# Four gate products and a second weight conversion moved into the attention loop of a fused attention and two-layer expert kernel

## The chip, the cores and the metric

The kernel runs on one core of a Trainium2 chip, as one program. The metric is the device time of one execution in microseconds. The engines are TensorE (PE, with its weight loads as PEld), VectorE (DVE), ScalarE (ACT), GpSimd (POOL) and SyncE (SP), whose queue issues the transfers.

## What is computed

Attention with rotary positions over 2 x 8 heads of 576 tokens and 64 dimensions, then a gated layer (512 to 1536 and back) over the 1152 tokens, then eight experts (512 to 1024 and back), all of them run for every token and weighted by a matrix that is normalised by rows and columns in turn.

```python
q_rot, k_rot = rotate(q), rotate(k)
attn = softmax(q_rot @ k_rot^T / 8)
x = heads_to_tokens(attn @ v)                      # 1152 x 512

g = x @ w_gate                                     # 512 x 1536
x = (g * sigmoid(g) * (x @ w_val)) @ w_out         # back to 1152 x 512

P = exp(x @ moe2_w_gate - max)                     # 1152 x 8
for _ in range(8):
    P /= P.sum(1); P /= P.sum(0); P *= 1152 / 8
out = sum(P[:, e] * (relu(x @ w1[e]) @ w2[e]) for e in range(8))
```

## The kernel before

Everything is float32. Each operand of a large product is split into a high part (rounded to the format that PE multiplies fast) and a low part (what the rounding left), and `mm3` (L145) issues three matmuls for one product: high by high (L148), high weights by low activations (L149), low weights by high activations (L150). Splitting the gated layer's weights is the work of `convert` (L103): a transfer on SP's queue (L114), an absolute value on ACT (L120), two DVE steps (L122, L123), a third (L126), the high part on ACT (L129), two more on DVE (L130, L132), and a subtraction (L66) and an addition (L136) that finish the low part. Outside attention all of a 1024-column unit goes at once and the last two are DVE's; inside attention it goes in halves of 512 columns, and the last two are POOL's.

**Attention** takes the heads in eight pairs, four for each batch. A pair has nine steps, one for each tile of scores: step 9n + u computes the scores of tile u of pair n (`scores`, L257), and DVE takes their row maximum (`row_max`, L262). One step later ACT takes the exponential (`exps`, L278), two steps later PE transposes it (`turn`, L297), which DVE or ACT copies out (`turned`, L312). The products with the values (`values`, L364) of the first four tiles and of the last five follow at steps given by `VALUES`, as do `rest`, `inverse` and `spread`, which turn the remainders and the inverse row sums. `summed` (L373) multiplies the two on DVE, and `finish` splits the result into `xh` (ACT, L379) and `xl` (L66). A dictionary `plan` keeps each of these calls under a step and a slot; `SLOTS` is the order of the slots within one step, and the steps run from -1 to 80. PE, ACT, POOL and SP execute the calls in this order; DVE's order is left to the scheduler. The last scores are those of step 71; the steps from 72 to 80 finish the last pair. Scores lie in a PSUM pool `ps_s` of two tiles with two banks each; transposes and values have two banks each, in `ps_t` and `ps_v`.

**Conversions in attention.** `CONVERSIONS` gives the step at which each half unit of the gate weights begins. Its load stands four steps before, and its stages 0 to 8 steps after:

```python
CONVERSIONS = (18, 32)
for i, t0 in enumerate(CONVERSIONS):
    f, half = divmod(i, 2)
```

So unit 0 is converted within attention, one half at step 18 and the other at step 32.

**The gated layer** (`gated`) has twelve units `f` of 128 columns, with gate and value weights side by side, and three chunks `c` of 384 tokens. `gv(f, c)` computes the gate product `pg` and the value product `pv`, 4 x 3 matmuls each, in two banks of a pool `ps` with eight, which is opened when attention's pools are closed. ACT takes the SiLU (L520), DVE the product with `pv` (L521), ACT the high part `uh` (L522) and DVE the low part `ul` (L66). Units 1 and 2 are converted first, and unit f + 2 when unit f begins. The output products `po` follow, and then the experts: `w1_tile` (12 matmuls, read by L591 on ACT and L592 on DVE) and `w2_tile`. The order of these instructions on each engine is the scheduler's, by its own estimate of times.

Of the kernel before, what the change touches and what calls it, by code (L numbers as in the profile page):

```python
# [10 lines left out]
F32 = mybir.dt.float32  # L11
# [5 lines left out]
PSUM = bass.MemoryType.PSUM  # L17
# [5 lines left out]
CH = 384  # L23
NC = NT // CH
KD = DM // 128
# [19 lines left out]
VALUES = ((1, 1, 3, 4, 4), (1, 2, 2, 4, 4))  # L45
SUMMED = (7, 6)
ACT_TURNS = (0, 2, 6)
CONVERSIONS = (18, 32)
WARM = 20
SCALE = float(1.0 / np.sqrt(D))  # L50

# [5 lines left out]
def fused(ctx, tc, qk, v, rope, wgv, wo, wg2, w1, w2, out):  # L57
    nc = tc.nc

    def pool(name, bufs=1, space=None, stack=ctx, **kw):  # L60
        if space is not None:
            kw["space"] = space
        return stack.enter_context(tc.tile_pool(name=name, bufs=bufs, **kw))
# [75 lines left out]
    def load_w64(src):  # L139
        hi, lo = new_w()  # L140
        for _ in convert(src, hi, lo, wide=True):
            pass
        return hi, lo

    def mm3(ps, w, wsl, x, xsl, first, last):  # L145
        wh, wl = w
        xh, xl = x
        nc.tensor.matmul(ps, wh[wsl], xh[xsl], start=first, stop=False)  # L148
        nc.tensor.matmul(ps, wh[wsl], xl[xsl], start=False, stop=False)  # L149
        nc.tensor.matmul(ps, wl[wsl], xh[xsl], start=False, stop=last)  # L150


    def attention(xT, W):
        with ExitStack() as st:
            inp.append(pool("inp", bufs=2, stack=st))
            ap_ = pool("att", stack=st)
# [5 lines left out]
            pt = pool("pt", bufs=1, stack=st)  # L162
            sm = pool("sm", bufs=4, stack=st)
            xf_p = pool("xf", bufs=2, stack=st)
            ps_s = pool("ps_s", bufs=2, space=PSUM, stack=st)
            ps_t = pool("ps_t", bufs=2, space=PSUM, stack=st)
            ps_v = pool("ps_v", bufs=2, space=PSUM, stack=st)

# [272 lines left out]
            for i, t0 in enumerate(CONVERSIONS):  # L441
# [6 lines left out]
                    at(t0 + t, slot, next, parts_)  # L448
                at(t0 + 8, "pool", next, parts_, None)


            first, later, half = slice(0, 256), slice(256, S), 288
            for x in blocks:
# [42 lines left out]
            assert not plan  # L496


    def gated(x, x2, ps, W, W1):
        nonlocal cvp  # L500
        with ExitStack() as st:
            cvp = pool("cvp", bufs=2, stack=st)
            up = pool("up", stack=st)
            tp = pool("tp", bufs=2, stack=st)
            uh = [up.tile([128, NT], F32R, name=f"uh{f}") for f in range(KF)]
            ul = [up.tile([128, NT], F32R, name=f"ul{f}") for f in range(KF)]

            def gv(f, c):
                if f not in W:
                    W[f] = load_w64(wgv[f])  # L510
                w = W[f]
                ts = slice(c * CH, c * CH + CH)
                pg = ps.tile([128, 512], F32, tag="a", name="pg")[:, 0:CH]
                pv = ps.tile([128, 512], F32, tag="a", name="pv")[:, 0:CH]
                for o, dst in ((0, pg), (512, pv)):
                    for kk in range(KD):
                        mm3(dst, w, (slice(None), slice(o + kk * 128, o + kk * 128 + 128)),
                            x, (slice(None), kk, ts), kk == 0, kk == KD - 1)
                sg = tp.tile([128, CH], F32, tag="sg", name="sg")
                nc.scalar.activation(out=sg, in_=pg, func=AF.Silu)  # L520
                nc.vector.tensor_tensor(out=sg, in0=pv, in1=sg, op=ALU.mult)  # L521
                nc.scalar.copy(out=uh[f][:, ts], in_=sg)  # L522
                sub(ul[f][:, ts], sg, uh[f][:, ts])

            order = [(f, c) for f in range(KF) for c in range(NC)]
            for f in range(2):
                if f not in W:
                    W[f] = load_w64(wgv[f])
            for n, (f, c) in enumerate(order):
                if c == 0 and f + 2 < KF and f + 2 not in W:  # L530
                    W[f + 2] = load_w64(wgv[f + 2])
                gv(f, c)
            O = {}
            nc.sync.dma_start(out=wr, in_=wg2)
            nc.scalar.copy(out=wg[:, :, 0], in_=wr)
            sub(wg[:, :, 1], wr, wg[:, :, 0])

            def o_unit(i):
                if i * 8 < KD * KF and i not in O:
                    O[i] = load_w64(wo[:, i * WU:(i + 1) * WU])  # L540

            o_unit(0)
            o_unit(1)
            xh, xl = x2
            for d in range(KD):
                for c in range(NC):
                    if d == KD - 1 and c < 2:
                        W1[0, c] = load_w(w1[0, :, c * WU:(c + 1) * WU])
                    ts = slice(c * CH, c * CH + CH)
                    po = ps.tile([128, 512], F32, tag="a", name="po")[:, 0:CH]  # L550
                    for kk in range(KF):
                        i, o = divmod(d * KF + kk, 8)
                        o_unit(i + 1)
                        mm3(po, O[i], (slice(None), slice(o * 128, o * 128 + 128)),
                            (uh[kk], ul[kk]), (slice(None), ts), kk == 0, kk == KF - 1)
                    nc.scalar.copy(out=xh[:, d, ts], in_=po)
                    sub(xl[:, d, ts], po, xh[:, d, ts])


    def experts(x, ps, W1):  # L560
        nonlocal cvp
        cvp = None
        inp.append(pool("inp", bufs=4))
# [17 lines left out]

        def w1_tile(e, c, f, hh, hl):
            ts = slice(c * CH, c * CH + CH)
            po = ps.tile([128, 512], F32, tag="a", name="p1")[:, 0:CH]
            i, o = divmod(f, 2)
            for kk in range(KD):
                q = o * 512 + kk * 128
                mm3(po, W1[e, i], (ALLP, slice(q, q + 128)), x, (ALLP, kk, ts), kk == 0, kk == KD - 1)
                if e == 0:
                    gate_step()  # L590
            nc.scalar.activation(out=hh[:, f], in_=po, func=AF.Relu)  # L591
            nc.vector.scalar_tensor_tensor(out=hl[:, f], in0=po, scalar=0.0, in1=hh[:, f].bitcast(F32),  # L592
                                           op0=ALU.max, op1=ALU.subtract)

        def w2_tile(e, c, t, hh, hl):
            po = ps.tile([128, 512], F32, tag="a", name="p2")
            tl = slice(t * 128, t * 128 + 128)
            for f in range(KF2):
                i, o = divmod(f, 2)
                wh, wl = W2[e, i]  # L600
                ws = slice(o * 512, o * 512 + 512)
                nc.tensor.matmul(po, hh[:, f, tl], wh[:, ws], start=f == 0, stop=False)  # L602
                nc.tensor.matmul(po, hh[:, f, tl], wl[:, ws], start=False, stop=False)  # L603
                nc.tensor.matmul(po, hl[:, f, tl], wh[:, ws], start=False, stop=f == KF2 - 1)  # L604
            t = c * 3 + t
            if e == 0:
                nc.vector.tensor_scalar(out=acc[:, t], in0=po, scalar1=Pm[:, t, e:e + 1], scalar2=None, op0=ALU.mult)
            else:
                nc.vector.scalar_tensor_tensor(out=acc[:, t], in0=po, scalar=Pm[:, t, e:e + 1], in1=acc[:, t],  # L609
                                               op0=ALU.mult, op1=ALU.add)  # L610
            if e == E - 1:
                nc.sync.dma_start(out=out[t * 128:t * 128 + 128, :], in_=acc[:, t])

        def gate():
# [2 lines left out]
            lt = ep.tile([2 * E, NT], F32, name="lt")  # L617
            for c in range(NC):
                ts = slice(c * CH, c * CH + CH)
                pl = ps.tile([128, 512], F32, tag="a", name="plt")  # L620
                for kk in range(KD):
                    nc.tensor.matmul(pl[0:2 * E, 0:CH], wgf[:, kk], xh[:, kk, ts], start=kk == 0, stop=False)
                    nc.tensor.matmul(pl[0:2 * E, 0:CH], wgf[:, kk], xl[:, kk, ts], start=False, stop=kk == KD - 1)
                nc.scalar.copy(out=lt[:, ts], in_=pl[0:2 * E, 0:CH])
                yield
            pt = ps.tile([128, 512], F32, tag="a", name="pt")
            for t in range(NTT):
                nc.tensor.transpose(pt[:, t * 16:t * 16 + 16], lt[:, t * 128:t * 128 + 128], ident[0:16, 0:16])
            lg = ep.tile([128, NTT, E], F32, name="lg")
# [2 lines left out]
            mx = ep.tile([128, 1], F32, name="mx")  # L632
            nc.vector.tensor_reduce(out=mx, in_=lg, axis=AX.XY, op=ALU.max)
            yield
            pm = ps.tile([128, 512], F32, tag="a", name="pm")
            nc.tensor.transpose(pm[0:1, 0:128], mx, ident)
            m1 = ep.tile([1, 1], F32, name="m1")
            nc.vector.tensor_reduce(out=m1, in_=pm[0:1, 0:128], axis=AX.X, op=ALU.max, negate=True)
            yield
            pb = ps.tile([128, 512], F32, tag="a", name="pb")  # L640
            nc.tensor.matmul(pb[:, 0:1], ones[0:1, :], m1, start=True, stop=True)
            nb = ep.tile([128, 1], F32, name="nb")
            nc.vector.tensor_copy(out=nb, in_=pb[:, 0:1])
# [4 lines left out]
            for _ in range(8):  # L648
# [2 lines left out]
                nc.vector.reciprocal(out=rs, in_=rs)  # L651
                nc.vector.tensor_tensor(out=Pm, in0=Pm, in1=rs.unsqueeze(2).to_broadcast([128, NTT, E]), op=ALU.mult)
                yield
                pc = ps.tile([128, 512], F32, tag="a", name="pc")
                nc.tensor.matmul(pc[:, 0:NTT * E], ones, Pm.rearrange("p t e -> p (t e)"), start=True, stop=True)
                nc.vector.tensor_reduce(out=cs, in_=pc[:, 0:NTT * E].rearrange("p (t e) -> p e t", e=E),
                                        axis=AX.X, op=ALU.add)
# [41 lines left out]

    make_identity(nc, ident)  # L700
    nc.gpsimd.memset(ones, 1.0)
    xT = new_x()
    W = {}
    attention(xT, W)
    ps = pool("ps", bufs=8, space=PSUM)
    x2 = new_x()
    W1 = {}
    gated(xT, x2, ps, W, W1)
    experts(x2, ps, W1)


# [54 lines left out]
```

## Time and profile before

| | us |
|---|---|
| runs | 1208.04, 1212.86, 1212.77 |
| median of the runs | 1212.77 |
| profiled execution | 1212.68 |
| its span, first to last instruction | 1210.60 |
| PE busy in the span | 1193.5 |
| DVE busy | 542.0 |
| ACT busy | 334.7 |
| POOL busy | 90.5 |

Busy time of PE is from the start of a matmul to its modelled end, and these overlap from one matmul to the next. So the time of one matmul in a row of them is read from the distance of their starts. A busy share is a mean over stages; what a stage waits for is read from the waits and from the order of time in that stage. Attention ends at about 178 us, the gated layer at about 407, and the rest is the experts.

### The profile page before, as it was taken

The numbers are of one execution on the slowest core, as the hardware profiler recorded it, in microseconds if no ns is written. First come the engines' busy times: TensorE is split into PE (matmuls) and PEld (weight loads), VectorE is DVE, ScalarE is ACT, GpSimd is POOL, SyncE is SP. The second block draws the span as 40 slices with busy tenths as digits, with TensorE's granted clock in tenths as the row PEclk, the third lists the DMA queues.
The fourth block names the chain that finished last, engine by engine and source line by source line (L and its number), as shares of the span: only waits on it lengthen the run. The fifth ranks groups of instructions, "written<-read, shape, count | busy, mean of one in ns | idle before, by whom it ended". The sixth has DMA issues, their size and how long they took to land.

```text
span 1210.6 us, 15264 instructions
## 1 busy us (share of the span) xinstructions
PE 1193.5 (99%) x6456; PEld 1074.7 (89%) x6456; DVE 542.0 (45%) x850; ACT 334.7 (28%) x599; POOL 90.5 (7%) x86
## 2 busy tenths in 40 slices
PE   7999999999999999999999999999999999999998
PEld 6666669999999999899899999989989989998997
DVE  7699868998742453232232332332323233233221
ACT  4556544443411412121131221212202112122110
POOL 5468400000000000000000000000000000000000
PEclk7899999999999999999999999999999999999999
DMA  4767503332211301010120220210102012020001
GB/s 158 207 163 187 144 25 116 120 125 87 88 53 57 135 1 53 30 58 19 52 70 1 70 70 1 70 68 3 49 22 70 15 56 70 1 70 1 9 18 52
DMA packets 24115, 80.52 MB, mean 67 GB/s; under 512 B 4272, under 2 KB 4784, under 8 KB 21872
## 3 DMA queue, kind: packets, MB, share of 16 engines
q1 hardware_dynamic: 24048, 79.56, 21.2%
q8 instruction: 50, 0.82, 0.3%
q14 instruction: 17, 0.14, 0.0%
HBM read 64.80 MB, written 2.36 MB: 55 GB/s over the span
## 4 chain that ended last, share of the span: by engine, by line
PE 94%; DVE 4%; DMA 1%; ACT 1%; issue 0%; SPq 0%; DVEq 0%; ACTq 0%
PE p L148 11%; PE p L150 11%; PE p L149 11%; PE p L603 11%; PE p L604 11%; PE p L602 11%; PE s L257 4%; PE pv L364 3%; PE t L297 2%; PE po L150 2%; PE po L149 2%; PE po L148 2%; PE pg L150 2%; PE pg L148 2%; PE pv L150 2%; PE pg L149 2%
## 5 line engine op out<-in xcount | busy, mean ns | idle before, releaser
L148 PE MATMUL p<-xh,wh 128*128 128x384 f32 x768 | 257.7, 336 | 0.0
L150 PE MATMUL p<-xh,wl 128*128 128x384 f32 x768 | 256.8, 334 | 0.0
L149 PE MATMUL p<-xl,wh 128*128 128x384 f32 x768 | 256.7, 334 | 0.0
L604 PE MATMUL p<-wh,hl 128*128 128x512 f32 x576 | 224.4, 390 | 0.0
L603 PE MATMUL p<-wl,hh 128*128 128x512 f32 x576 | 224.4, 390 | 0.0
L602 PE MATMUL p<-wh,hh 128*128 128x512 f32 x576 | 224.0, 389 | 0.0
L591 ACT ACTIVATE hh<-p 128x384 fp32r<-128x384 f32 x192 | 94.2, 491 | 370.6 <-PE p L150 370.6
L592 DVE SCALAR_TENSOR_TENSOR hl<-p,hh 128x384 fp32r<-128x384 f32 x192 | 106.8, 556 | 188.7 <-ACT hh L591 188.6
L609 DVE SCALAR_TENSOR_TENSOR acc<-p,Pm,acc 128x512 f32<-128x512 f32 x63 | 47.3, 750 | 254.1 <-PE p L604 254.1
L148 PEld LDWEIGHTS p<-xh,wh 128*128 128x128 f32 x768 | 144.2, 188 | 0.9
L149 PEld LDWEIGHTS p<-xl,wh 128*128 128x128 f32 x768 | 144.2, 188 | 0.6
L150 PEld LDWEIGHTS p<-xh,wl 128*128 128x128 f32 x768 | 144.1, 188 | 0.0
L99 ACT CAST wh<-raw 128x1024 fp32r<-128x1024 f32 x64 | 67.2, 1053 | 249.3 <-PE p L604 197.7
L604 PEld LDWEIGHTS p<-wh,hl 128*128 128x128 f32 x576 | 108.1, 188 | 22.5
L603 PEld LDWEIGHTS p<-wl,hh 128*128 128x128 f32 x576 | 108.1, 188 | 22.2
L602 PEld LDWEIGHTS p<-wh,hh 128*128 128x128 f32 x576 | 108.1, 188 | 22.1
L66 DVE TENSOR_TENSOR wl<-raw,wh 128x1024 fp32r<-128x1024 f32 x64 | 78.2, 1224 | 78.4 <-ACT wh L99 76.5
L262 DVE TENSOR_REDUCE ng<-s 128x1 f32<-128x576 f32 x72 | 53.5, 749 | 15.6 <-PE s L257 10.6
L278 ACT ACTIVATE p<-s,ng 128x576 f32<-128x576 f32 x64 | 47.6, 743 | 40.1 <-DVE ng L262 39.8
L148 PE MATMUL pg<-xh,wh 128*128 128x384 f32 x144 | 48.9, 339 | 3.1 <-ACT wh L129 2.4
L149 PE MATMUL pg<-xl,wh 128*128 128x384 f32 x144 | 48.5, 337 | 0.0
L150 PE MATMUL pg<-xh,wl 128*128 128x384 f32 x144 | 48.5, 337 | 0.0
(126 smaller groups left out, 1400.6 us busy)
## 6 DMA issues: line engine op xcount, KB each, us to landing
raw<-in_w SPq DMA_DIRECT2D x64, 512.0 KB, 3.9
raw<-in_wgv SPq DMA_DIRECT2D x11, 1024.0 KB, 4.9
x<-in_qk SPq DMA_DIRECT2D x15, 576.0 KB, 4.6
raw<-in_wo SPq DMA_DIRECT2D x6, 1024.0 KB, 4.9
x<-hl SPq DMA_DIRECT2D x42, 144.0 KB, 3.4
x<-hl SPq DMA_DIRECT2D x14, 288.0 KB, 3.3
v<-in_v SPq DMA_DIRECT2D x8, 320.0 KB, 5.0
out<-acc SPq DMA_DIRECT2D x9, 256.0 KB, 2.0
```

Of the source, the lines that this page charges most:

```text
L66: (eng or nc.vector).tensor_tensor(out=out_, in0=a, in1=hi.bitcast(F32), op=ALU.subtract)
L99: nc.scalar.copy(out=hi, in_=raw)
L148: nc.tensor.matmul(ps, wh[wsl], xh[xsl], start=first, stop=False)
L149: nc.tensor.matmul(ps, wh[wsl], xl[xsl], start=False, stop=False)
L150: nc.tensor.matmul(ps, wl[wsl], xh[xsl], start=False, stop=last)
L257: nc.tensor.matmul(ps[:, c, o:o + ks.stop - ks.start], q, k, start=t == 0, stop=t == len(terms) - 1)
L262: nc.vector.tensor_reduce(out=R[n, u], in_=SC[n, u][:, :, 0:288], axis=AX.XY, op=ALU.max, negate=True)
L591: nc.scalar.activation(out=hh[:, f], in_=po, func=AF.Relu)
L592: nc.vector.scalar_tensor_tensor(out=hl[:, f], in0=po, scalar=0.0, in1=hh[:, f].bitcast(F32), op0=ALU.max, op1=ALU.subtract)
L602: nc.tensor.matmul(po, hh[:, f, tl], wh[:, ws], start=f == 0, stop=False)
L603: nc.tensor.matmul(po, hh[:, f, tl], wl[:, ws], start=False, stop=False)
L604: nc.tensor.matmul(po, hl[:, f, tl], wh[:, ws], start=False, stop=f == KF2 - 1)
```

## The change

Two more conversions stand in the loop, so unit 1 of the gate weights is converted at steps 50 and 63 of attention. At steps 72 to 75 a new function `gate_half` is planned in the slot `pe3`; it computes the gate and the value product of chunk 0 for unit 0 (72 and 73) and for unit 1 (74 and 75). Their results lie in score tiles: the score pool is now `duos`, opened before attention and kept until the end. The gated layer's other banks are a pool `singles` of four, opened when attention's pools are closed, and `bank` hands out its banks and the halves of `duos` tiles in turn. In `gated`, the results of chunk 0 of units 0 and 1 are read first; then unit f + 2 is converted when unit f begins, and units 0 and 1 compute chunks 1 and 2 alone. All other places that took a bank of `ps` now call `bank`.

```diff
-CONVERSIONS = (18, 32)
+CONVERSIONS = (18, 32, 50, 63)
+AHEAD = (72, 73, 74, 75)
...
-            ps_s = pool("ps_s", bufs=2, space=PSUM, stack=st)
+            ps_s = duos
...
+            for i, t0 in enumerate(AHEAD):
+                at(t0, "pe3", gate_half, xT, W, G, *divmod(i, 2))
...
+    def gate_half(x, W, G, f, half):
+
+        if half == 0:
+            G[f] = duos.tile([128, 2, 512], F32, tag="s", name="g")
+        for kk in range(KD):
+            o = half * 512 + kk * 128
+            mm3(G[f][:, half, 0:CH], W[f], (slice(None), slice(o, o + 128)), x, (slice(None), kk, slice(0, CH)),
+                kk == 0, kk == KD - 1)
...
             def gv(f, c):
-                if f not in W:
-                    W[f] = load_w64(wgv[f])
-                w = W[f]
                 ts = slice(c * CH, c * CH + CH)
-                pg = ps.tile([128, 512], F32, tag="a", name="pg")[:, 0:CH]
-                pv = ps.tile([128, 512], F32, tag="a", name="pv")[:, 0:CH]
-                for o, dst in ((0, pg), (512, pv)):
-                    for kk in range(KD):
-                        mm3(dst, w, (slice(None), slice(o + kk * 128, o + kk * 128 + 128)),
-                            x, (slice(None), kk, ts), kk == 0, kk == KD - 1)
+                if c == 0 and f in G:
+                    pg, pv = (G[f][:, i, 0:CH] for i in range(2))
+                else:
+                    w = W[f]
+                    pg, pv = bank("pg")[:, 0:CH], bank("pv")[:, 0:CH]
+                    for o, dst in ((0, pg), (512, pv)):
+                        for kk in range(KD):
+                            mm3(dst, w, (slice(None), slice(o + kk * 128, o + kk * 128 + 128)),
+                                x, (slice(None), kk, ts), kk == 0, kk == KD - 1)
...
-            order = [(f, c) for f in range(KF) for c in range(NC)]
-            for f in range(2):
-                if f not in W:
-                    W[f] = load_w64(wgv[f])
-            for n, (f, c) in enumerate(order):
-                if c == 0 and f + 2 < KF and f + 2 not in W:
+            for f in G:
+                gv(f, 0)
+            for f in range(KF):
+                if f + 2 < KF:
                     W[f + 2] = load_w64(wgv[f + 2])
-                gv(f, c)
+                for c in range(int(f in G), NC):
+                    gv(f, c)
...
+    duos = pool("duos", bufs=2, space=PSUM)
+    singles = duo = None
+    turns = [0]
+
+    def bank(name):
+
+        nonlocal duo
+        i = turns[0] % 8
+        turns[0] += 1
+        if i < 4:
+            return singles.tile([128, 512], F32, tag="a", name=name)
+        if i % 2 == 0:
+            duo = duos.tile([128, 2, 512], F32, tag="s", name=name)
+        return duo[:, i % 2]
+
     xT = new_x()
-    W = {}
-    attention(xT, W)
-    ps = pool("ps", bufs=8, space=PSUM)
+    W, W1, G = {}, {}, {}
+    attention(xT, W, G)
+    singles = pool("singles", bufs=4, space=PSUM)
```

## Rows read from the trace of the kernel before

**Rows 1.** The page, part 1: busy us, share of the span, instructions

```profile
PE 1193.5 (99%) x6456; PEld 1074.7 (89%) x6456; DVE 542.0 (45%) x850; ACT 334.7 (28%) x599; POOL 90.5 (7%) x86
```

**Rows 2.** Waits of PE over the span: in total, times, longest

```profile
PE s L257 <- ACT hl L209: 5.1, 1, 5.1
PE pg L148 <- ACT wh L129: 2.4, 1, 2.4
```

**Rows 3.** PE in order of time: start, us, operation, idle time before it

```profile
178.21 0.41 PE L148 MATMUL pg<-xh,wh 128*128 128x384 f32 x1 [0.68 <-DVE xf L373]
...
190.79 0.33 PE L148 MATMUL pg<-xh,wh 128*128 128x384 f32 x1
...
192.69 0.34 PE L149 MATMUL pv<-xl,wh 128*128 128x384 f32 x1
195.47 0.69 PE L148 MATMUL pg<-xh,wh 128*128 128x384 f32 x1 [2.44 <-ACT wh L129]
...
198.66 0.33 PE L150 MATMUL pg<-xh,wl 128*128 128x384 f32 x1
```

**Rows 4.** Stretches: PE, PEld, DVE, ACT, POOL busy, granted clock, DMA share, GB/s

```profile
170.00:178.20 8.20, 7.52 (x48) 3.65 (x49) 4.27 (x12) 2.15 (x7) 1.41 (x1) 1.00 0.00 0
195.10:198.40 3.30, 2.93 (x9) 2.94 (x10) 3.30 (x5) 0.73 (x2) 0.00 (x0) 0.50 0.44 104
```

**Rows 5.** Order of time: the first load behind attention, the low parts on DVE

```profile
178.21 18.08 SPq L114 DMA_DIRECT2D raw<-in_wgv  x3
...
194.72 1.21 DVE L136 TENSOR_TENSOR wl<-cv,raw 128x1024 fp32r<-128x1024 f32 x1
...
199.31 1.23 DVE L136 TENSOR_TENSOR wl<-cv,raw 128x1024 fp32r<-128x1024 f32 x1
```

**Rows 6.** Order of time: the last exponential, PE's `values` behind it

```profile
170.48 0.75 ACT L278 ACTIVATE p<-s,ng 128x576 f32<-128x576 f32 x1
...
171.64 0.65 PE L364 MATMUL pv<-q,v 64*64 64x256 f32 x4
```

**Rows 7.** Order of time: the half conversion of step 32, first and last

```profile
91.19 0.68 ACT L120 ACTIVATE cv<-raw 128x512 f32<-128x512 f32 x1
...
109.06 1.33 POOL L136 TENSOR_TENSOR wl<-cv,raw 128x512 fp32r<-128x512 f32 x1
```

**Rows 8.** Order of time: PE and weight loads where tile shapes change

```profile
157.96 0.76 PE L364 MATMUL pv<-p,v 128*64 128x320 f32 x4
158.65 0.80 PE L257 MATMUL s<-x,x 128*128 128x288 f32 x4
...
160.20 1.30 PE L364 MATMUL pv<-p,v 128*64 128x320 f32 x8
161.43 0.40 PE L257 MATMUL s<-hl,bd 128*128 128x288 f32 x1
...
173.93 0.20 PEld L349 LDWEIGHTS t<-ident,iv 128*128 128x128 f32 x2 [0.49 <-issue]
```

**Rows 9.** Stretches as in 4: attention's pairs 1 to 6

```profile
41.45:59.69 18.24, 18.24 (x129) 12.80 (x127) 14.75 (x28) 11.37 (x26) 9.03 (x9) 1.00 0.65 174
59.69:79.74 20.05, 18.82 (x129) 12.83 (x127) 19.26 (x33) 11.48 (x27) 12.83 (x11) 1.00 0.62 161
79.74:99.85 20.11, 18.99 (x132) 12.95 (x131) 19.49 (x34) 11.95 (x28) 14.67 (x13) 1.00 0.72 198
99.85:116.92 17.07, 17.07 (x125) 12.44 (x126) 14.17 (x30) 11.84 (x28) 12.07 (x11) 1.00 0.65 175
116.92:135.71 18.79, 18.29 (x128) 12.77 (x127) 15.88 (x29) 11.74 (x28) 13.96 (x13) 1.00 0.61 156
135.71:153.96 18.25, 18.25 (x129) 12.80 (x127) 14.93 (x28) 10.55 (x25) 4.63 (x5) 1.00 0.44 104
```

**Rows 10.** Groups of instructions: busy us, mean ns, idle before

```profile
L521 DVE TENSOR_TENSOR sg<-pv,sg 128x384 f32<-128x384 f32 x35 | 19.4, 553 | 11.0 <-PE pv L150 10.9
L592 DVE SCALAR_TENSOR_TENSOR hl<-p,hh 128x384 fp32r<-128x384 f32 x192 | 106.8, 556 | 188.7 <-ACT hh L591 188.6
```

More of the change, by code (lines that the diff above doesn't have):

```diff
@@ L150, in mm3, with attention @@
         nc.tensor.matmul(ps, wl[wsl], xh[xsl], start=False, stop=last)
-    def attention(xT, W):
+    def attention(xT, W, G):
         with ExitStack() as st:
@@ L496, in attention, with gated @@
             assert not plan
-    def gated(x, x2, ps, W, W1):
+    def gate_half(x, W, G, f, half):
[5 more added lines that the diff above has]
+                kk == 0, kk == KD - 1)
+    def gated(x, x2, W, W1, G):
         nonlocal cvp
@@ L549, in gated @@
                     ts = slice(c * CH, c * CH + CH)
-                    po = ps.tile([128, 512], F32, tag="a", name="po")[:, 0:CH]
+                    po = bank("po")[:, 0:CH]
                     for kk in range(KF):
@@ L557, in gated, with experts @@
                     sub(xl[:, d, ts], po, xh[:, d, ts])
-    def experts(x, ps, W1):
+    def experts(x, W1):
         nonlocal cvp
@@ L583, in w1_tile @@
             ts = slice(c * CH, c * CH + CH)
-            po = ps.tile([128, 512], F32, tag="a", name="p1")[:, 0:CH]
+            po = bank("p1")[:, 0:CH]
             i, o = divmod(f, 2)
@@ L595, in w2_tile @@
         def w2_tile(e, c, t, hh, hl):
-            po = ps.tile([128, 512], F32, tag="a", name="p2")
+            po = bank("p2")
             tl = slice(t * 128, t * 128 + 128)
@@ L619, in gate @@
                 ts = slice(c * CH, c * CH + CH)
-                pl = ps.tile([128, 512], F32, tag="a", name="plt")
+                pl = bank("plt")
                 for kk in range(KD):
@@ L625, in gate @@
                 yield
-            pt = ps.tile([128, 512], F32, tag="a", name="pt")
+            pt = bank("pt")
             for t in range(NTT):
@@ L634, in gate @@
             yield
-            pm = ps.tile([128, 512], F32, tag="a", name="pm")
+            pm = bank("pm")
             nc.tensor.transpose(pm[0:1, 0:128], mx, ident)
@@ L639, in gate @@
             yield
-            pb = ps.tile([128, 512], F32, tag="a", name="pb")
+            pb = bank("pb")
             nc.tensor.matmul(pb[:, 0:1], ones[0:1, :], m1, start=True, stop=True)
@@ L653, in gate @@
                 yield
-                pc = ps.tile([128, 512], F32, tag="a", name="pc")
+                pc = bank("pc")
                 nc.tensor.matmul(pc[:, 0:NTT * E], ones, Pm.rearrange("p t e -> p (t e)"), start=True, stop=True)
@@ L701, in fused @@
     nc.gpsimd.memset(ones, 1.0)
+    duos = pool("duos", bufs=2, space=PSUM)
[10 more added lines that the diff above has]
+        return duo[:, i % 2]
     xT = new_x()
-    W = {}
-    attention(xT, W)
-    ps = pool("ps", bufs=8, space=PSUM)
+    W, W1, G = {}, {}, {}
+    attention(xT, W, G)
+    singles = pool("singles", bufs=4, space=PSUM)
     x2 = new_x()
-    W1 = {}
-    gated(xT, x2, ps, W, W1)
-    experts(x2, ps, W1)
+    gated(xT, x2, W, W1, G)
+    experts(x2, W1)
 def _tables():
```

## Prediction

> **What bounds the kernel now.** I read the page's busy shares first: TensorE (PE) is busy for 99% of the span, VectorE (DVE) for 45% [rows 1]. So only what PE waits for, or what is added to its stream, moves the end. The list of PE's waits comes next: one of 5.1 us at the start, which the change doesn't touch, then 2.4 us in the gate products for `wh` from ScalarE (ACT) [rows 2]; the others are smaller. The third view is the order of time on PE around the 2.4 us. Unit 0 of the gate weights, converted during attention, gives PE 72 products from 178.21 to 190.79, which is 0.1747 us each. Then come 12 products of unit 1 that need only its high part, then nothing until 195.47, 2.44 us after the last had ended [rows 3]. [...] So the ten products from 195.47 to 198.66 take 3.19 us [rows 3] and not 1.75. The gap with its slow clock costs 2.44 + 1.44 = **3.88 us**.
>
> What PE stands for is the conversion of units 1 and 2. Its first transfer is issued at 178.21, when attention's last result is out. Unit 1's low part is written by 194.72 + 1.21 = 195.93 and unit 2's by 199.31 + 1.23 = 200.54, which is 17.7 and 22.3 us after that issue [rows 5].
>
> The last main view is the stretch in which the change puts the first products, the end of attention. It would pay to put them there if PE were idle. PE is busy 7.52 of 8.20 us [rows 4], and the only wait of size is the 0.68 us at 178.21 for DVE's last product [rows 3].
>
> **The change part by part.** *Products moved into attention.* Four half products of 12 matmuls, 4 x 12 x 0.1747 = 8.39 us of PE time, move from behind 178.21 to steps 72 to 75. The same 48 matmuls go on the same engine, which has no gaps there: moved alone they cost and bring nothing, and attention ends 8.39 us later. DVE's and ACT's work in those steps (copies of turned probabilities, inverse sums) runs beside them. The 0.68 us wait stays, I take it: the new pool of four banks lies where attention's other PSUM pools were, and can wait for the same last reader. If it goes, 0.68 us are won.
>
> New waits on PE: a score tile must be free, and `wl` of unit 1 must be written. Behind a waiting product stand the next `turn`, `rest` and `values` on PE, and behind those DVE's copies. The last exponential is over at 170.48 + 0.75 = 171.23, and the first product comes behind the `values` that start at 171.64 [rows 6]: both tiles are free in time. For `wl`, the slower of the earlier halves took from 91.19 to 110.39, from its first ACT to the end of its last POOL instruction, 19.2 us [rows 7]. The second half of unit 1 starts at step 63, whose scores lie near 154 [rows 9], so it is done near 173; its product stands last of the four, at about 172.2 + 3 x 2.1 + 3 us of attention's own work = 181.5. Eight us are left: zero, and a `wl` later than that would cost what it is late.
>
> *More changes of the array's shape.* `values` uses tiles of 128x64 and 64x64, the rest 128x128. The products at steps 74 and 75 stand between steps of `values`, which adds two changes, one into 128x128 and one out again. Four `values` matmuls up to a change take 0.69 us (157.96 to 158.65) and eight take 1.23 (160.20 to 161.43) [rows 8], so a change costs 0.69 - (1.23 - 0.69) = 0.15 and two cost **+0.30 us**. The bounds: zero, as PE shows no idle time there, and two waits of the weight load at a change, 2 x 0.49 = 0.98 [rows 8]. I take 0.30, as it is the spacing of the same instructions. [...]
>
> *Unit 1 converted in attention.* Two halves, at steps 50 and 63, each with a 512 KB load, two ACT, five DVE and two POOL instructions. Two such halves, at steps 18 and 32, are in the kernel before, and attention cut at the first score reduction of each pair of heads prices them. Pairs 2 and 3, with a half each, take 20.05 and 20.11 us, and DVE is busy 19.26 and 19.49 of it. Pair 4 behind them takes 17.07. Pairs 1, 5 and 6, without one, take 18.24, 18.79 and 18.25, with DVE at 14.75 to 15.88 [rows 9]. Pairs 2 to 4 together are 57.23 us against 3 x 18.43, so two halves cost **+1.94 us**, net of what is caught up. Bounds: zero, if DVE's idle 2.9 and 3.3 us in pairs 5 and 6 take it all, and 2 x 1.65 = 3.30 without the catching up. I take 1.94, from the same instructions in the same loop. The DVE work itself is 4.2 us per half, the difference of the two groups' DVE time.
>
> Queues: the loads stand on SP's queue at steps 46 and 59. Behind the second is `load_v` of pair 7, first needed eight steps later, some 16 us by a pair's nine steps: zero. POOL's two instructions per half stand ahead of `finish` of pairs 5 and 6, whose low parts are read only behind attention, and POOL is busy 4.63 us in pair 6 [rows 9]: zero. ACT's high copy waits for DVE and holds back the next exponential; that is in the measured 1.94.
>
> *The gap for unit 1* goes with its slow clock: **-3.88 us**. What is late next is unit 2, whose transfer is now the first behind attention. PE then has the other two chunks of units 0 and 1, 4 x 24 x 0.1747 = 16.8 us, and 12 products of unit 2 with the high part alone, 2.1 us: the low part must be there 18.9 us after the issue. The first unit took 17.7 before, and DVE has one more chunk to finish first, two instructions of 0.55 [rows 10]: 18.8. So there is no wait, with 0.1 us to spare. Later units follow 12.6 us of PE work apart, as before, when none of them was waited for.
>
> *Banks in pairs.* A pair of banks is reused when both are read. A tile of the experts' first product is 12 matmuls, 2.1 us of PE work, and its last reader takes 0.56 [rows 10], so it is read long before the six tiles between have passed: zero. Without that cover it would cost one reader, 0.6 us, per pair.
>
> **Sum** against the profiled execution, 1212.68 us (a span of 1210.6 and 2.08 around it): 1212.68 - 3.88 + 1.94 + 0.30 = 1211.04, so **1211.0**. The runs shown are 1208.04 to 1212.86 with a median of 1212.77, so the profiled one lies at their upper end.
>
> **Rivals.** (a) *Attention takes the conversion for nothing, and the products fill the last wait.* DVE has room in pairs 5 to 7, and POOL little to do in pairs 6 and 7; against it, the neighbours of pairs 2 and 3 had room too. 1212.68 - 3.88 + 0.30 - 0.68 = **1208.4**. That the products fill idle time, which is what their place is good for, is in this case alone, and for 0.68 us, as the trace has no more.
>
> (b) *Unit 2 stands where unit 1 stood*, slower than before. Units 2 and 3 are converted side by side on DVE, as 1 and 2 were; if the low part of unit 2 comes more than 18.9 us after its issue, PE stands again, and the second unit of before took 22.3. With the same gap and slow clock, 1212.68 + 1.94 + 0.30 = **1214.9**. The margin of 0.1 us speaks for it; against it, unit 2 is first in the program and unit 3 comes behind two chunks.
>
> (c) *DVE sets the pace of the last pairs*, and each half costs its whole 4.2 us: 1212.68 - 3.88 + 0.30 + 8.4 = **1217.5**. Pairs 2 and 3 speak against it: with DVE at 96% they lost 1.65 each.
>
> **How the numbers follow.** The forecast has 0.52, with a range of its own of 1208.8 to 1213.1 by the bounds of the conversion and of the changes of shape; (a) 0.20, (b) 0.20, (c) 0.06, something else 0.02. The range goes from (a) less some of the spread of the runs, 1206.5, to a little above (b), 1216.0, and leaves (c) out. A measurement of this kernel can tell about 0.5%, 6.1 us, from no change. No case is faster by so much, and slower by it is only (c) with a wait for unit 2 on top; faster 0.05 and slower 0.04 are for these and for the spread of the runs, same has 0.91.
>
> **What would show it.** Right: no wait of PE over 0.5 us between 190 and 230 and a granted clock of 1.00 there; attention's last product some 10.6 us later, near 188; pairs 5 to 7 longer by about 1 us for each half. Wrong: a wait of the first products for `wl` or a score tile; PE waiting for `wh` or `wl` of unit 2, with a clock of 0.50 behind it (b); pairs 5 and 6 as long as before, or no wait of PE where the gate products follow attention (a); DVE at 96% of pairs over 20 us (c).

## The result and the profile after

The changed kernel takes **1215.84 us** (median of 8 runs, 1214.87 to 1223.96) against 1208.18 us for the kernel before (8 runs, 1206.41 to 1212.86). The ratio is 1.0063, with a 95% interval of 1.0041 to 1.0086: slower by 0.6%, and the interval leaves out no change. The forecast was 1211.0, a little faster, which would have counted as no change. The profiled execution took 1223.96 us, 11.28 more than that of before.

To find the 11.28 us, three marks are read from the order of time in both traces: the first score reduction of pair 2 in attention, the first product of the gated layer's output, and the last matmul. They cut the span into a start, a stretch A (most of attention and the gate products) and a stretch B (output products, router and experts).

| us | before | after | difference |
|---|---|---|---|
| start to pair 2 | 59.69 | 63.01 | +3.32 |
| A: pair 2 to the first output product | 272.44 | 270.21 | -2.23 |
| of it, to the last `values` | 117.40 | 127.58 | +10.18 |
| of it, from there on | 155.03 | 142.64 | -12.39 |
| B: first output product to last matmul | 874.25 | 884.65 | **+10.40** |
| behind the last matmul, up to the time | 6.30 | 6.09 | -0.21 |

The +3.32 is not the change's: E3, E4, E6 and E7, which run the changed attention too, begin pair 2 at 54.5 to 59.9 us (see the last section). Without it 7.96 us are left, near the 7.66 between the medians. So where the change was meant to act it brought 2.23 us, and in B, which it hardly seems to touch, it lost 10.40.

The page of after, part 1, and PE's waits over the whole span (waited for, total, times, longest):

```profile
PE 1200.4 (98%) x6456; PEld 1076.7 (88%) x6456; DVE 539.3 (44%) x853; ACT 334.7 (27%) x601; POOL 96.6 (8%) x90
```

```profile
PE s L258 <- ACT hl L210: 5.1, 1, 5.1
...
PE plt L640 <- ACT lt L636: 1.5, 1, 1.5
PE p L149 <- DVE hl L604: 1.2, 1, 1.2
...
PE p L648 <- DVE mx L645: 0.9, 1, 0.9
PE p L614 <- DVE acc L621: 0.8, 1, 0.8
...
PE pg L149 <- DVE xf L374: 0.7, 1, 0.7
...
PE p L149 <- DVE m L650: 0.4, 1, 0.4
PE p L149 <- DVE cs L668: 0.3, 1, 0.3
```

Against [rows 2], `pg <- ACT wh` with its 2.4 us is gone. New behind attention are six of the lines shown, 5.1 us together: the router waits for `lt` and `mx`, and the experts' products `p` wait for `hl` and `acc` and for the router's `m` and `cs`. The line `p L149 <- DVE m L650` is odd: an expert's product, which reads `x` and `w1`, waits for a reduction of the router's maximum, of which it needs nothing. PE is busy 6.9 us longer than in [rows 1] with as many instructions (6456). The start's clock has part in that, so here is B alone, before and then after (window, length, busy time of PE, PEld, DVE, ACT, POOL, granted clock, DMA share, GB/s):

```profile
332.10:1206.40 874.30, 874.30 (x4518) 803.76 (x4516) 269.54 (x424) 171.83 (x278) 0.00 (x0) 1.00 0.13 43
```

```profile
333.20:1217.90 884.70, 879.27 (x4518) 806.33 (x4516) 267.43 (x423) 171.28 (x278) 0.00 (x0) 1.00 0.13 42
```

Before, PE is never idle in B; after, it is idle for 5.4 us, and for as many instructions it is busy 5.0 us longer. So about half of the loss is slower work and not idle time.

PE in order of time (start, us, operation, idle time before it), at the join of attention and the gate products, then in the router, in the first experts, and at the end:

```profile
190.25 0.76 PE L365 MATMUL pv<-q,v 64*64 64x320 f32 x4
191.70 0.41 PE L149 MATMUL pg<-xh,wh 128*128 128x384 f32 x1 [0.69 <-DVE xf L374]
...
418.63 0.73 PE L640 MATMUL plt<-ident,lt 16*128 16x16 f32 x9 [1.54 <-ACT lt L636]
...
421.53 0.37 PE L648 MATMUL p<-ident,mx 128*1 128x128 f32 x1 [0.93 <-DVE mx L645]
422.27 0.69 PE L149 MATMUL p<-xh,wh 128*128 128x384 f32 x1 [0.37 <-DVE m L650]
...
436.58 0.45 PE L149 MATMUL p<-xh,wh 128*128 128x384 f32 x1 [1.17 <-DVE hl L604]
...
1212.52 0.50 PE L614 MATMUL p<-wh,hh 128*128 128x512 f32 x1 [0.85 <-DVE acc L621]
```

Stretches of after (length, busy time of PE, PEld, DVE, ACT, POOL, granted clock, DMA share, GB/s): pairs 5 and 6, the join, and a stretch behind the router:

```profile
120.21:140.43 20.22, 18.97 (x131) 12.97 (x131) 19.60 (x33) 11.68 (x28) 14.78 (x13) 1.00 0.67 175
140.43:157.49 17.06, 17.06 (x125) 12.43 (x126) 14.17 (x29) 11.82 (x29) 7.10 (x7) 1.00 0.54 136
191.70:215.00 23.30, 23.30 (x134) 23.30 (x135) 20.23 (x29) 13.67 (x21) 0.00 (x0) 1.00 0.37 137
421.10:427.90 6.80, 6.00 (x18) 5.25 (x19) 2.13 (x9) 2.13 (x3) 0.00 (x0) 0.50 0.59 217
```

Behind the join PE has no idle time and a clock of 1.00: the gap of [rows 3] and the slow stretch of [rows 4] are gone. They have a successor, though. Behind the waits in the router the clock is 0.50 for 6.8 us (421.10 to 427.90). 18 matmuls at 0.1747 us [rows 3] would be 3.14 us (an estimate, as three of them are the router's and smaller); PE was busy 6.00.

### The profile page after: what moved, and what is told of

It is laid out like the page before. It is cut to its first block, busy times and chain, and to the rows that moved or that the text cites. A ratio compares the mean times of both kernels' runs of the same rounds, so it can differ in the third digit from the quotient of the medians.

```text
span 1222.2 us, 15334 instructions
## 1 busy us (share of the span) xinstructions
PE 1200.4 (98%) x6456; PEld 1076.7 (88%) x6456; DVE 539.3 (44%) x853; ACT 334.7 (27%) x601; POOL 96.6 (8%) x90
## 4 chain that ended last, share of the span: by engine, by line
PE 93%; DVE 5%; ACT 1%; issue 1%; DMA 0%; SPq 0%; DVEq 0%; ACTq 0%
PE p L149 11%; PE p L151 11%; PE p L150 11%; PE p L616 11%; PE p L615 11%; PE p L614 11%; PE s L258 4%; PE pv L365 3%; PE pg L149 3%; PE pg L151 3%; PE pg L150 3%; PE t L298 2%; PE po L149 2%; PE po L150 2%; PE po L151 2%; PE pv L149 1%
## 5 line engine op out<-in xcount | busy, mean ns | idle before, releaser
L149 PE MATMUL p<-xh,wh 128*128 128x384 f32 x764 | 257.1, 337 | 1.9 <-DVE hl L604 1.2
L149 PEld LDWEIGHTS p<-xh,wh 128*128 128x128 f32 x764 | 144.2, 189 | 3.8 <-DVE hl L604 1.5
L100 ACT CAST wh<-raw 128x1024 fp32r<-128x1024 f32 x64 | 67.3, 1052 | 219.1 <-PE p L616 158.2
L149 PE MATMUL pg<-xh,wh 128*128 128x384 f32 x200 | 66.9, 334 | 0.7 <-DVE xf L374 0.7
L150 PE MATMUL pg<-xl,wh 128*128 128x384 f32 x200 | 66.8, 334 | 0.0
L151 PE MATMUL pg<-xh,wl 128*128 128x384 f32 x200 | 66.8, 334 | 0.0
```

Source lines behind the costliest of these rows:

```text
L100: nc.scalar.copy(out=hi, in_=raw)
```

## The experiments

**Theories.** T1: the loss lies in how banks are handed out. Since the change, four of the eight banks come as two tiles `duos` of two banks each, and both halves of such a tile are ordered as one. T2: it lies in what was moved into attention (conversion and products), by what that shifts behind it. T3: it is the program's changed order alone. In the texts on record before the runs, T1 is called theory S and T2 theory L. The table gives A and B of each kernel, cut as above, from one profiled execution each; all times of kernels are medians, with their ratio to the kernel before from the same chip (1210.38 for E1 to E4, 1211.26 for E5 to E8) and its 95% interval.

| kernel | what it has | A | B | ratio |
|---|---|---|---|---|
| before | | 272.44 | 874.25 | |
| after | all | 270.21 | 884.65 | 1.0063 |
| E1 | conversion alone | 269.41 | 874.25 | 0.9972 (0.9952 to 0.9993) |
| E2 | shared tiles alone | 274.47 | 881.33 | 1.0083 (1.0053 to 1.0112) |
| E3 | all, no shared tiles | 270.24 | 874.33 | 0.9980 (0.9960 to 1.0000) |
| E4 | all, one half of each tile | 270.20 | 874.33 | 0.9979 (0.9958 to 1.0000) |
| E5 | products alone, no shared tiles | 275.86 | 874.41 | 1.0016 (0.9998 to 1.0034) |
| E6 | shared up to the output products | 270.24 | 877.51 | 1.0008 (0.9988 to 1.0028) |
| E7 | shared in router and experts | 270.20 | 878.86 | 1.0014 (0.9994 to 1.0035) |
| E8 | E1, and banks waited for singly | 268.69 | 874.25 | 0.9953 (0.9931 to 0.9975) |

### E1: unit 1 converted in attention, nothing else (against the kernel before)

```diff
-CONVERSIONS = (18, 32)
+CONVERSIONS = (18, 32, 50, 63)
```

> The kernel before with the second conversion in attention alone (steps 50 and 63), with no product moved and its eight single banks. In the changed kernel attention's pairs 5 to 7 were 1.1 us longer than before and the gap of 3.88 us for unit 1 was gone. Theory S (two halves of one PSUM tile are ordered as one tile, which makes the waits in the experts): nothing of that is here, so -3.88 + 1.1 = -2.8 us, some 1205.4, ratio 0.998, and no wait of PE between 400 and 460. Theory L (the earlier gated layer shifts the experts' conversions into the router, whatever the banks): waits of PE for lt, mx and hl between 400 and 460 and a stretch of clock 0.50, ratio 1.002 to 1.006.

1207.81 us. A falls by 3.03 and B is the same to 0.01. Pair 2 to the last `values` is 118.45, 1.05 more than before: that is the price of two halves. From there to the first output product it is 150.96, 4.07 less: that is the gap with its slow clock. So the whole gain comes from the conversion; no product has to be moved for it.

### E2: only the shared tiles (compared with the kernel before)

The changed kernel's pools and `bank`, with unit 1 converted behind attention and no product planned in it. The edit is one of the changed kernel:

```diff
-CONVERSIONS = (18, 32, 50, 63)
-AHEAD = (72, 73, 74, 75)
+CONVERSIONS = (18, 32)
+AHEAD = ()
...
+            for f in range(2):
+                if f not in W:
+                    W[f] = load_w64(wgv[f])
```

> The kernel before with the changed bank pools alone: four single banks and two tiles of two banks handed out by halves; one unit converted in attention and no product moved. Theory S: the gap for unit 1 stays and the waits of the experts appear, +6 to +9 us, some 1216, ratio 1.005 to 1.008, PE waiting between 400 and 460 for lt, mx, m or hl and near the end for acc. Theory L: banks make no difference, ratio 1.000, no wait there.

1221.97 us, slower than the kernel before, and by a little more than the ratio of 1.005 to 1.008 that was expected. B is 7.08 longer with no product planned in attention. The rest is in A (+2.03). Of it 0.79 lies before the last `values`: in PE's order of time the scheduler has put nine `pg` matmuls of unit 0 (1.57 us) among attention's last steps by itself, so this kernel is not quite free of moved products. The other 1.25 lies behind: unit 1 is late as before, by 3.8 us and not 2.4, and the clock behind it is 0.50 for 6.8 us and not 3.4 (its fastest run has a mean granted clock of 0.991, E1's 0.994). PE's waits from 400 to 470 us:

```profile
PE p L149 <- ACT lt L639: 2.1, 1, 2.1
PE p L149 <- DVE hl L607: 1.2, 1, 1.2
...
```

An expert's product `p` and the router's `lt` have no data in common; the first row again shows a product waiting for a reader of something else. T2 can hardly explain this kernel: but for those nine matmuls nothing was moved.

### E3 and E4: the whole change without shared halves (against the changed kernel)

E3 closes `duos` once the four moved products are read, and gives its four banks out singly:

```diff
-    duos = pool("duos", bufs=2, space=PSUM)
-    singles = duo = None
+    duo_stack = ExitStack()
+    duos = pool("duos", bufs=2, space=PSUM, stack=duo_stack)
+    singles = pairs = None
...
-        if i < 4:
-            return singles.tile([128, 512], F32, tag="a", name=name)
-        if i % 2 == 0:
-            duo = duos.tile([128, 2, 512], F32, tag="s", name=name)
-        return duo[:, i % 2]
+        if i >= 4 and pairs is None:
+            duo_stack.close()
+            pairs = pool("pairs", bufs=4, space=PSUM)
+        return (singles if i < 4 else pairs).tile([128, 512], F32, tag="a", name=name)
...
-    singles = pool("singles", bufs=4, space=PSUM)
+    singles = pool("singles", bufs=4, space=PSUM, side="right")
```

> The changed kernel, with the tiles of two banks given up once the moved products are read: the single banks are opened on the other side of PSUM, and four more single banks take the place of the two tiles. Theory S: attention and the gated layer as in the changed kernel, the experts as before: -2.2 us, some 1206, ratio 0.998, no wait of PE between 400 and 460 and none for acc at the end. Theory L: the experts stay as in the changed kernel, 1215, ratio 1.006.

E4 keeps `duos` to the end, but hands out a whole tile for one result, so that there are six places and not eight:

```diff
-        i = turns[0] % 8
+        i = turns[0] % 6
...
-        if i % 2 == 0:
-            duo = duos.tile([128, 2, 512], F32, tag="s", name=name)
-        return duo[:, i % 2]
+        return duos.tile([128, 2, 512], F32, tag="s", name=name)[:, 0]
```

> The changed kernel, with a whole tile of two banks handed out for each bank of those two tiles, of which one half is left empty: six places in turn, and no tile has two users. Theory S: as with the tiles given up, some 1206, ratio 0.998, since sharing is the cause. If it is the turn of places that costs (a place comes free only when both halves are read), six places are tighter still: as slow as the changed kernel or slower, ratio 1.006 or more.

1206.18 and 1206.11 us, and B is 874.33 in both, 0.08 more than before. E4 has two banks fewer than any other kernel here and loses nothing, so the number of banks isn't what the changed kernel lacks. What is left of the difference is that two results share one tile. All of the 10.40 us goes with it. A stays at 270.2, so the change without its shared tiles is worth 2.2 us. PE's waits of E3, whole span, all lines:

```profile
PE s L258 <- ACT hl L210: 6.4, 1, 6.4
PE s L258 <- ACT p L279: 2.8, 4, 1.0
PE t L185 <- POOL ones L713: 1.1, 1, 1.1
PE pv L365 <- DVE p L313: 0.8, 2, 0.5
PE pg L149 <- DVE xf L374: 0.7, 1, 0.7
PE t L350 <- DVE iv L337: 0.6, 1, 0.6
```

None of the six waits is left. With all that was moved still in attention, B is as before: that refutes T2.

### E5: the moved products alone (against E3)

```diff
-CONVERSIONS = (18, 32, 50, 63)
-AHEAD = (72, 73, 74, 75)
+CONVERSIONS = (18, 32)
+AHEAD = (72, 73)
...
+            W[1] = load_w64(wgv[1])
             for f in G:
```

> The moved products alone: those of unit 0 at steps 72 and 73, unit 1 converted behind attention as before, no tile shared (the tiles of two banks are given up once the products are read). Stage A runs from pair 2's first score reduction to the first output product (before 272.44 us, changed kernel 270.21), stage B from there to the last matmul (before 874.25, changed kernel 884.65). If attention's end has no idle PE time, the 24 products only change places, the gap for unit 1 grows by the 4.16 us of work that is no longer there to cover it, and the added change of shape costs some 0.4: A 277 to 279, B 874.3, ratio 1.004 to 1.006. If they fill idle time, A is 272 or less.

1211.46 us. A is 3.42 longer than before, less than expected. Moving unit 0's two half products shortens the work behind attention by 24 matmuls of 0.1747, 4.19 us, and the conversion of units 1 and 2 begins later by as much, so PE stands longer. In order of time:

```profile
185.61 0.41 PE L149 MATMUL pg<-xh,wh 128*128 128x384 f32 x1 [0.69 <-DVE xf L374]
...
195.68 0.44 PE L149 MATMUL pg<-xh,wh 128*128 128x384 f32 x1 [1.48 <-ACT wh L130]
...
201.82 0.44 PE L149 MATMUL pg<-xh,wh 128*128 128x384 f32 x1 [3.79 <-ACT wh L130]
```

The wait for `wh` is 1.48 + 3.79 = 5.3 against 2.44 [rows 3]. It grows by 2.8 and not by 4.19, as the second `wh` is there 201.82 - 185.61 = 16.2 us after the first product behind attention here and 195.47 - 178.21 = 17.3 in [rows 3]; that was not forecast. Up to the last `values` this kernel needs 121.64, 4.24 more than before; less the 4.19 of the products, 0.05 is left. At steps 72 and 73, where it breaks no row of `values`, a moved product costs nothing beyond itself.

### E6 and E7: where the sharing costs (compared with E3)

E6 shares tiles up to the output products and then goes over to single banks; E7 does the opposite. Both edits are made to the changed kernel; this is E6's, and E7's follows:

```diff
+        if pairs is not None:
+            return pairs.tile([128, 512], F32, tag="a", name=name)
...
+    duo_stack.close()
+    pairs = pool("pairs", bufs=4, space=PSUM)
     experts(x2, W1)
```

> The changed kernel with shared tiles up to the output products and eight single banks in the experts. The last two output products share a tile, so the last one still stands behind two of the router's products in PE's order, but the router's tiles share with none. Stages A and B as above: A 270.2. If the displaced output product carries the loss (it brings ACT's and DVE's conversions of the experts' weights into the router's chain), B is 880 or more and the waits for lt and mx stay; if the router's own sharing carries it, B is 876 or less.

```diff
+        if i >= 4 and shared is not None:
+            if i % 2 == 0:
+                duo = shared.tile([128, 2, 512], F32, tag="s", name=name)
+            return duo[:, i % 2]
...
+    pair_stack.close()
+    shared = pool("shared", bufs=2, space=PSUM)
     experts(x2, W1)
```

> The opposite: single banks up to the output products, then two shared tiles of two banks in the experts, at the same turn as in the changed kernel. All output products come before the router, as before. A 270.2. If the router's own sharing carries the loss, B is 880 or more, with waits for m, hl, cs and at the end acc; if the displaced output product carries it, B is 876 to 878 with those waits of some 2 to 3 us in all. The two kernels' losses should add up to the changed kernel's 10.4, but for the slow clock, which comes or doesn't.

E6: 1210.28 us, B 3.26 longer than in the kernel before. E7: 1213.84 us, B 4.61 longer. Both parts cost; in either kernel B lies between the two cases expected. PE's waits of E6 from 398 to 450 us, then of E7 from 398 us to the end:

```profile
PE plt L634 <- DVE xl L67: 1.4, 1, 1.4
PE pm L648 <- DVE mx L645: 1.3, 1, 1.3
```

```profile
PE p L149 <- DVE hl L604: 1.2, 1, 1.2
PE p L614 <- DVE acc L621: 0.8, 1, 0.8
PE p L149 <- DVE m L650: 0.4, 1, 0.4
PE p L149 <- DVE cs L668: 0.3, 1, 0.3
```

E6's two waits are 2.7 of its 3.26, E7's four 2.7 of its 4.61; beside these waits PE shows no idle time in B, so the rest lies in matmuls whose starts are further apart, and wasn't followed further. Together 7.87, and neither kernel has a clock of 0.50 in that place (the mean granted clock of their fastest runs is 0.994, that of the changed kernel's 0.992). The changed kernel has both kinds of wait within a few us of each other, and it alone has the 6.8 us at 0.50. The 10.40 - 7.87 = 2.5 us that are left fit the excess of that stretch: 6.00 - 3.14 = 2.9 us of slower PE work. E2, which shares in both parts, has no 0.50 there and loses 7.08, points the same way. No run shows the slow stretch apart from its waits, so this share is argued and not shown.

T3 can be looked at in the compiled instruction list of the changed kernel. Here are four of PE's instructions with their waits (left out: those between):

```
L149 MATMUL po_4117<-uh0_2419,wh_3923 128x384 [waits DVE_49]
...
L151 MATMUL p1_4325<-xh_2408,wl_4114 128x384
L648 MATMUL p1_4325<-ident_58,mx_4321 1x128 [waits DVE_49]
L149 MATMUL p1_4325<-xh_2408,wh_4113 128x384 [waits DVE_49]
```

The numbers are those of tiles. Line 648 is the router's transpose, in one half of tile 4325; in the other half, an expert's sum over four steps is under way. Its next step now waits for DVE, which has to read the router's half first. That is the 0.37 before 422.27 above. The order was changed too: in before, E1, E3, E4 and E7 all 432 matmuls of the output products stand ahead of the router, while in after and E6 the last 36, whose tile's other half has yet to be read, stand behind 12 products of the experts and 15 of the router. In E2 all 432 stand ahead, too, and B is 7.08 longer all the same. The changed order is thus a result of the sharing, and only one of the ways in which it costs; T3 isn't a cause beside it. It makes PE wait for ACT in the router. ACT in order of time, before and then after:

```profile
408.36 2.95 ACT L99 CAST wh<-raw 128x1024 fp32r<-128x1024 f32 x3
...
414.50 0.47 ACT L624 COPY lt<-plt 16x384 f32<-16x384 f32 x1 [0.16 <-PE plt L623]
```

```profile
413.79 0.47 ACT L568 CAST xh<-po 128x384 fp32r<-128x384 f32 x1
414.16 1.99 ACT L100 CAST wh<-raw 128x1024 fp32r<-128x1024 f32 x2
416.05 0.83 ACT L636 COPY lt<-plt 16x384 f32<-16x384 f32 x2
416.79 0.47 ACT L603 ACTIVATE hh<-p 128x384 fp32r<-128x384 f32 x1
417.17 1.03 ACT L100 CAST wh<-raw 128x1024 fp32r<-128x1024 f32 x1
418.11 0.46 ACT L636 COPY lt<-plt 16x384 f32<-16x384 f32 x1
```

Casts of the experts' weights (L99, now L100) stand ahead of the third copy of `lt` in both. Before, that copy waits for PE; after, PE waits 1.54 for it. Of the 48 matmuls of the list that stood between the last output product and the router's transposes of `lt`, 27 now stand ahead of that product, and the 21 left don't cover ACT's work.

Whether the two halves of a `duos` tile, two banks, need an order between them isn't shown: no run left them without one. The compiled kernel orders by the tile, and here that costs 10.40 us in B.

### E8: E1, and each bank waits for its own readers alone

Wanted was the 0.69 before the first gate product as well, which no kernel so far had lost:

```diff
-CONVERSIONS = (18, 32)
+CONVERSIONS = (18, 32, 50, 63)
...
-    ps = pool("ps", bufs=8, space=PSUM)
+    ps = pool("ps", bufs=8, space=PSUM, reuse_waits="tile")
```

> The second conversion in attention alone, on eight single banks, each of which waits only for the users of its own bank and not for all of attention's pools. Stage A was 269.41 with the conversion alone. If PE's 0.7 us wait for DVE's last product at the start of the gated layer is the pool's and not the data's, it goes: A 268.4 to 268.8, B 874.25, ratio 0.996 to 0.997; if the data are what is waited for, A 269.4.

**1203.93 us**, ratio 0.9953 (0.9931 to 0.9975): faster than both kernels, and the best of these. A is 0.72 shorter than E1's, B the same. PE's waits, whole span, all but the first two lines, which are as in E3:

```profile
...
PE t L184 <- POOL ones L701: 1.1, 1, 1.1
PE pv L364 <- DVE p L312: 0.8, 2, 0.5
PE t L349 <- DVE iv L336: 0.6, 1, 0.6
```

The line with `pg` is gone: the first gate product had waited for the readers of all of attention's banks, and not for those of its own.

## Why the prediction failed, step by step

**The step that failed** is "Banks in pairs", with its price of zero. It asked only when a pair of banks is used again, and found six tiles between. An order between the two halves of one pair it didn't consider. There is one, and it is paid where two results with different rhythms come to lie in one tile: output product and router, router and expert. The price named for "without that cover", 0.6 us per pair, is of the right kind (single waits of 0.3 to 1.5 us), but it stood as a case that wouldn't come, so neither the sum nor a rival held it. Measured: +10.40 us in B against a forecast of 0; E3 and E4 take all but 0.08 of it away.

**The gap for unit 1**, -3.88: right. Its slow clock is the 0.50 of [rows 4]. E1 has -4.07.

**The conversion in attention**, +1.94: right in kind, too high. E1 has +1.05, within the bounds of zero and 3.30. In the changed kernel pair 5, with the first half, takes 20.22, 1.43 more than in [rows 9], but pair 6 behind it takes 17.06 against 18.25 there. So all but 0.24 is caught up in the next pair. The half in pair 7 adds 0.83 from its first score to its last (16.51 against 15.68). The working let one pair catch up for two halves, as pair 4 does in [rows 9]; here the first half had a pair of its own behind it.

**Two more changes of shape**, +0.30: there are four, and the price of one was about right. From pair 2 to the last `values` it is 10.18 more; less 8.39 for 48 products and 1.05 for the conversion, 0.74 is left. E5, whose products break no row of `values`, has 0.05 left over. The same `values` before, and then after with the moved products `g`:

```profile
174.47 2.37 PE L364 MATMUL pv<-p,v 128*64 128x320 f32 x14
```

```profile
183.06 0.75 PE L365 MATMUL pv<-p,v 128*64 128x320 f32 x2
183.74 0.45 PE L149 MATMUL g<-xh,wh 128*128 128x384 f32 x1
...
186.05 1.30 PE L365 MATMUL pv<-p,v 128*64 128x320 f32 x8
187.28 0.44 PE L149 MATMUL g<-xh,wh 128*128 128x384 f32 x1
...
189.56 0.76 PE L365 MATMUL pv<-p,v 128*64 128x320 f32 x4
```

The products of steps 74 and 75 break the row in two places, each with a change into 128x128 and one out again. So a change costs 0.74 / 4 = 0.18 us, an estimate from this remainder, near the 0.15 that the spacing of matmuls in [rows 8] gave and far from the 0.49 that the weight load waits there; the count of two was wrong.

**Products moved**: "alone they cost and bring nothing", right but for these changes of shape. E1, without them, is 0.83 us shorter in A than E3 with them. "If the 0.68 us wait goes": it stayed (0.69 at 191.70), as forecast; E8 shows what it was.

**Unit 2 not late**: right, with 1.5 us to spare and not 0.1: its low part is written at 208.60, 16.9 us after the issue at 191.69, and first read at 210.15. No wait of PE over 0.5 us behind 191.70 in the gate products, so (b) didn't happen. Its 1214.9 lies near the measured 1215.84 by chance: the time was lost 200 us later. The stated range was drawn up to 1216.0 for (b), so it is luck, too, that 1215.84 lies inside it. (a) is refuted, as the conversion isn't for nothing. (c) is too: DVE is busy 19.60 of 20.22 in pair 5, but the two halves together cost 1.05, not 8.4.

**The sum for A** was -3.88 + 1.94 + 0.30 = -1.64; measured is -2.23, and the whole change without shared tiles (E3) gives -2.20. The last product of attention came at 190.58 and not near 188; 3.32 of that is the start's slow clock. The forecast was thus good to 0.6 us on the stretch that it studied, in part by luck, since the conversion came 0.89 too high and the changes of shape 0.44 too low; and it was 10.4 us off on the stretch that it dismissed in a few sentences.

## What to carry to other kernels

Where an edit pools buffers into larger tiles, every later user of them can get new orders, as here: go through the pairs of results that will share a tile, along the whole kernel, and ask who reads the one before the other may be written; a shared tile whose halves go to results with different readers is the one to suspect. An edit that brings two things (here a conversion and moved products) should be priced as each alone: the conversion held the whole gain, and the products and their tiles all of the loss. Where the engine that bounds a kernel waits at a join of two stages, look at whether it waits for its own buffer or for the whole pool's.

## What was not expected of the hardware

The granted clock at the start differs between executions of one kernel. It falls to 0.50 after 11 to 14 us, and stays there for 13.7, 23.9, 27.3 or 34.1 us in the executions seen; pair 2 then starts at 54.5 to 54.8, 59.5 to 59.7, 59.6 to 59.9 or 62.9 to 63.0 us. The same stretch in E1 and in the kernel before, then a later one in the kernel before and after:

```profile
25.00:36.00 11.00, 10.86 (x71) 8.07 (x70) 8.22 (x15) 6.05 (x15) 8.65 (x8) 0.92 0.82 187
```

```profile
25.00:36.00 11.00, 11.00 (x44) 8.53 (x44) 6.62 (x13) 5.34 (x13) 6.98 (x7) 0.50 0.74 168
36.00:46.00 10.00, 10.00 (x65) 6.66 (x61) 5.91 (x13) 3.95 (x9) 2.30 (x4) 0.90 0.63 202
```

```profile
36.00:46.00 10.00, 10.00 (x43) 6.24 (x39) 3.02 (x6) 2.61 (x6) 1.94 (x2) 0.52 0.66 196
```

In the first, PE gets through 71 matmul records in 11 us at 0.92; in the second through 44 in as long at 0.50, with the same instructions in the same order (the two kernels differ only from step 46 on). Up to 8.5 us of the time hang on this, as much as on the change, and repeated runs of one kernel lie in steps that go with it (E8: 1203.4 to 1204.0 at a mean granted clock of 0.994, then 1206.9 to 1208.9 at 0.991 and 0.988). A single execution of this kernel can't show an effect of a few us; a cut behind the start, as in A and B, can: B of the kernel before, of E1 and of E8 is the same to 0.01 us. What decides the length of the slow stretch wasn't tried.
